# Forming the high and low parts of k at other places of an attention stage, and 25 idle products of 256 columns at its head

## The chip, the cores and the metric

The kernel runs on one core of one Trainium2 chip. The metric is the time of one execution on the device in microseconds (us), the median over repeated executions. The engines are TensorE (PE in the rows, with PEld for its weight loads), VectorE (DVE), ScalarE (ACT), GpSimd (POOL) and SyncE (SP), which here only issues transfers (DMAs).

## The reference

Three layers run one after the other in float32. The attention layer weighs with a sigmoid, not a softmax; a gated layer of eight experts and a dense layer with an exponential curve follow. This text is about the first one.

```python
# batch 4, heads 12, tokens S = 448, head size 64
scores = (q @ k.transpose) / sqrt(64) - log(S)
attn = 1 / (1 + exp(-scores))
attn_out = attn @ v
# then, on 1792 rows of 768: each row's best of 8 experts (768 -> 1024 -> 768), where x @ w_skip > 0,
# and at last (elu(x @ w_in)) @ w_out with 768 -> 2048 -> 768
```

## The kernel before, in words

**Numbers.** A float32 factor is given to TensorE as two rounded parts (type fp32r): a high part, which ScalarE casts (`split_qk`, line 239), and a low part, the rest, which VectorE subtracts (line 241). A product of two such factors takes three products of parts: high with high, high with low, low with high.

**Tiles.** Two heads lie side by side on the 128 partitions and make a pair; 4 x 6 = 24 pairs are worked through, n = 0 to 23, by the loop at line 660, with one more turn for what is left over. Two pairs make a group T: they share one load of q and of k (tiles `qr`, `kr`, `k_left`) and one set of parts: `qh`, `ql` of q and `kh`, `kl` of k, each 128 x 896 or 128 x 768, in two buffers. p = n % 2 says which pair of its group n is.

**A pair.** For each n the code runs c = 0 to 3 (line 692). At c = 0 come the scores of three blocks of 128 keys: `scores` (line 249) gives TensorE six products a block, in the order (kh, qh), (kh, ql), (kl, qh), each for two heads at once, and ScalarE the sigmoid of the block (`weigh`, line 244), which writes `at`. At c = 2 comes `mix` of the pair before (line 265): 24 or 12 float32 products into the one bank `po`; then `left_keys` (lines 281 and 291): the last 64 keys of both pairs, their sigmoid, and VectorE's copy of `po` to `xT` (line 296). At c = 3, in ten of the pairs from n = 8 on, `rows` (line 316) turns 128 finished tokens with six transposes into the tile `px`, and ScalarE copies them out (line 326). The blocks of scores, the left keys and `px` share a ring of three PSUM buffers (`pss`, line 194): what takes a buffer waits until the user three places before it was read.

**The parts of the next group** are formed in the group before it, at line 703: in the pair with p = 0 those of q, in the pair with p = 1 those of k, the high part at c = 1, the low part at c = 3. Only the first group's parts are formed ahead of the loop (lines 627 and 628).

**Beside this** VectorE rewrites 18 weight tiles of the dense layer (`narrow`, line 147: `sg`, `mg`, `mf`), six steps a tile, one, one, one and two steps at c = 0 to 3; each tile's load is issued a tile ahead (`wide_load`, line 145). From pair 19 on a generator (`sooner`, line 461) adds the small steps that choose experts; its last step is the first gather of rows by GpSimd (line 564).

**Order.** The order of TensorE, ScalarE and VectorE is the order of the code; each works through its list one by one. The transfers of SyncE and the steps of GpSimd are put in order by the planner. The loads of a group's q and k are issued one group ahead of the forming of their parts (line 680).

**The head.** `keep_warm` (line 205) gives TensorE products of zeros before any data is there: 21 of 384 columns, bfloat16.

Of the kernel before, what the change touches and what calls it, by code (L numbers as in the profile page):

```python
# [12 lines left out]
F32 = mybir.dt.float32  # L13
# [10 lines left out]
P = 128  # L24
# [67 lines left out]
def build(nc, tc, a):  # L92
# [3 lines left out]
    with ExitStack() as top:  # L96
# [80 lines left out]
        with ExitStack() as st:  # L177
# [16 lines left out]
            pss = pst.enter_context(tc.tile_pool(name="pss", bufs=3, space=PSUM))  # L194
# [7 lines left out]
            zero_b = xp.tile([P, 1, P], BF16, name="zero_b")  # L202
            nc.gpsimd.memset(zero_b, 0.0)

            def keep_warm(n):

                ps = pss.tile([P, 3, P], F32, name="idle", tag="ps")
                for _ in range(n):
                    nc.tensor.matmul(
                        ps, zero_b[:, 0], zero_b.to_broadcast([P, 3, P]), start=True, stop=True  # L210
                    )

            keep_warm(21)
            xT = xp.tile([P, NP, NT], F32, name="xT")
            lgT = xp.tile([P, RING * P], F32, name="lgT")

            def load(b, t, first=False):
                qr = qkp.tile([P, 2, S], F32, name="qr", bufs=3)
                kr = qkp.tile([P, 2, FULL * P], F32, name="kr")
                kl = qkp.tile([P, 2, LEFT], F32, name="k_left", bufs=3)  # L220
                if first:
                    for p in range(2):
                        nc.sync.dma_start(qr[:, p], q[b, t, :, p])
                        (nc.scalar, nc.sync)[p].dma_start(kr[:, p], k[b, t, :, p])
                else:
                    nc.sync.dma_start(qr, q[b, t])
                    nc.sync.dma_start(kr, k[b, t])
                nc.sync.dma_start(kl, k_left[b, t])
                return qr, kr, kl

            def split_tiles(raw):
                sizes = {"qh": S, "ql": S, "kh": FULL * P, "kl": FULL * P}
                return raw, [qkp.tile([P, 2, m], F32R, name=n) for n, m in sizes.items()]

            def split_qk(which, raw, parts, p=slice(None), hi=True, lo=True):
                r, (h, rest) = raw[which], parts[2 * which : 2 * which + 2]
                m = h.shape[2]
                if hi:
                    nc.scalar.copy(h[:, p], r[:, p, :m])
                if lo:  # L240
                    nc.vector.tensor_sub(rest[:, p], r[:, p, :m], h[:, p])

            def weigh(out, ps):
                nc.scalar.activation(out, ps, AF.Sigmoid, bias=bias, scale=QK_SCALE)  # L244
# [279 lines left out]
            def some_weights(pool, raws, splits):  # L524

                for _ in range(splits):
                    for w_t, n in ((whi_t, "whi"), (wlo_t, "wlo")):
                        w_t.append(pool.tile([P, WCH], F32R, name=f"{n}{len(w_t)}"))
                for _ in range(raws):
                    raw_t.append(pool.tile([P, WCH], F32, name=f"raw{len(raw_t)}"))  # L530
# [4 lines left out]
            def fetch(i, chunks, after=()):  # L535
                if i == NB:
                    return
                e = nc.values_load(
                    blk_e[i : i + 1, :1] if i else blk_0[:1],
                    engines=[mybir.EngineType.SP], min_val=0, max_val=E - 1,  # L540
                )
                for c in chunks:
                    src = (w1, w2)[c // 4][bass.ds(e, 1), c % 4].rearrange("o p f -> (o p) f")
                    dma = nc.sync.dma_start(raw_of(i, c), src)
                    for other in after:
                        tc.add_manual_dep(dma.ins, other.ins.name, SYNC)
# [65 lines left out]
            steps = B * NP  # L612
            raw = load(0, 0, True)
# [45 lines left out]
            nxt = None  # L659
            for n in range(steps + 1):  # L660
                b, hp = divmod(n, NP)
                T, p = divmod(n, 2)
                if n == steps - 1:
                    assert narrowed == 2 * FA
                    fetch(0, range(2))
                if n == steps:
                    qst.close()
                    wi1p = top.enter_context(tc.tile_pool(name="wi1p", reuse_waits="tile", bufs=1))
                    wi1 = wi1p.tile([P, DM], F32, name="wi1")
                    tokp = st.enter_context(tc.tile_pool(name="tokp", reuse_waits="tile", bufs=1))  # L670
                    some_weights(tokp, 2, 2)
                    fetch(0, range(2, 4), first_rows)
                    lg = logits(B - 1, None, range(KD - 2))
                if p == 0 and n < steps:
                    if n:
                        cur = nxt
                    if T + 1 < steps // 2:
                        nxt = split_tiles(nxt_raw)
                        if T + 2 < steps // 2:
                            nxt_raw = load(*divmod(T + 2, 3))  # L680
                    else:
                        nxt = None
                if p == 1 and T + 1 < steps // 2:
                    load_v(T + 1)
                at = atp.tile([P, 2 * FULL + 1, S], F32, name="at") if n < steps else None
                po = ps1.tile([P, 512], F32, name="po", tag="po") if n else None
                if m3 is not None and c0 + 1 < n:
                    nc.scalar.copy(wi0[0], m3)
                    nc.vector.tensor_sub(wi0[1], m3, wi0[0])
                    m3 = None  # L690
                turn = done_rows < LATE and hp > (b < B - 1) and (done_rows + 1) * P <= b * S
                for c in range(4):
                    now = (n, c)
                    first_splits(n, c)
                    for c2 in range(FULL):
                        if c == 0 and n < steps:
                            scores(at, c2, p, *cur[1])
                        if c == 2 and n:
                            mix(c2, n - 1, *prev, po)
                    if c == 2:  # L700
                        left_keys(n, cur, at, prev, po)
                    if nxt and n < steps and c in (1, 3):
                        split_qk(p, *nxt, hi=(c == 1), lo=(c == 3))
                    if turn and c == 3:
                        rows(done_rows)
                        done_rows += 1
                    if hp == 1 and b > 0 and c == 0:
                        logits(b - 1)
                    if hp == 1 and b > 0 and c in (2, 3):
                        m = min(4, b * S // P - done_lgt)  # L710
                        if m > 0 and b < B:
                            token_logits(done_lgt, m)
                            done_lgt += m
                    if now >= (SOON_STEP, 3):
                        for _ in range(2 + (n > SOON_STEP + 1)):
                            next(soon, None)
                    for _ in range((1, 1, 1, 2)[c] if n else 0):
                        if conv is None and narrowed < 2 * FA:
                            mf = cvp.tile([P, DM], F32, name="mf")
                            w = wides[narrowed % 2]  # L720
                            if narrowed + 1 < 2 * FA:
                                wide_load(wides[(narrowed + 1) % 2], narrowed + 1)
                            sg = cvp.tile([P, DM], I32, name="sg", bufs=1)
                            mg = cvp.tile([P, DM], I32, name="mg", bufs=1)
                            conv = narrow(mf, w, sg, mg, False)
                        if conv is not None and next(conv, 1):
                            if narrowed == 0:
                                m3, c0 = mf.rearrange("p (c f) -> p c f", c=KD), n
                            else:
                                nc.sync.dma_start((wi_d, wo_d)[narrowed % 2][narrowed // 2], mf)  # L730
                            narrowed += 1
                            conv = None
                prev = (vts.get(T), at)
# [554 lines left out]
        with ExitStack() as st:  # L1288
# [118 lines left out]
            steps = [(bi, f) for bi in range(len(blocks)) for f in range(KF2)]  # L1407
# [37 lines left out]
            for s, (bi, f) in enumerate(steps):  # L1445
# [13 lines left out]
                if bi + 1 < len(blocks):  # L1459
# [5 lines left out]
                    if f == 7:  # L1465
                        nxt = x_tiles(bi + 1)
# [55 lines left out]
```

## Time and profile before

| | us |
|---|---|
| median of three executions | 903.27 (902.49 to 905.52) |
| the profiled execution | 902.08 |
| its span, first to last instruction | 900.3 |
| PE busy in the span | 869.1 (97%) |
| DVE busy | 555.7 (62%) |
| ACT busy | 477.4 (53%) |

The attention stage fills about the first 170 us of the span; experts and dense layer fill the rest. The profile gives for every instruction its start from the beginning of the span, its duration and, where its engine sat idle before it, for how long and what ended the idle time. The mean granted TensorE clock over the span is 0.999 of full speed.

### The profile page before, as it was taken

Reading aid. Unit: us, or ns where it says so; the run is one execution under the profiler, and the core shown is the slowest. Engines: PE = TensorE matmul, PEld = TensorE weight load, DVE = VectorE, ACT = ScalarE, POOL = GpSimd, SP = SyncE. Lnnn points to the kernel's source line nnn. Section 1 sums busy time; section 2 is a strip of 40 time slices with the busy share of each in tenths; the row PEclk is TensorE's granted clock in tenths of the full one; section 3 lists DMA queues with packets and bytes.
Section 4 is the critical chain, followed back from the end, with each engine's and each line's share of the span. In section 5 each row is a group of like instructions: output and inputs, shape, how many; then the busy total and the mean of one; then the engine's idle time right before and its main releaser. Section 6 shows DMA issues by size and latency. Waiting matters only on the chain.

```text
span 900.3 us, 13676 instructions
## 1 busy us (share of the span) xinstructions
PE 869.1 (97%) x5202; PEld 703.9 (78%) x5202; DVE 555.7 (62%) x872; ACT 477.4 (53%) x680; POOL 82.1 (9%) x79
## 2 busy tenths in 40 slices
PE   8899999999999898998999999999999999999998
PEld 4444444699998787887888888888888888888997
DVE  4866767697666466885888886434344444344664
ACT  6767676555455465773545545434434434344664
POOL 1000000112110032332100000100000100000100
PEclk9999999999999999999999999999999999999999
DMA  9778785779956165955733430100000100000100
GB/s 314 260 258 298 260 308 188 258 281 410 360 187 223 55 284 216 410 203 198 245 103 96 118 106 19 71 1 18 18 18 19 71 1 1 1 1 18 54 1 36
DMA packets 37842, 134.71 MB, mean 150 GB/s; under 512 B 5082, under 2 KB 9306, under 8 KB 37746
## 3 DMA queue, kind: packets, MB, share of 16 engines
q1 hardware_dynamic: 33122, 114.26, 35.6%
q0 software_dynamic: 4480, 19.01, 5.9%
q8 instruction: 56, 0.92, 0.4%
q14 instruction: 40, 0.33, 0.1%
q10 hardware_dynamic: 144, 0.20, 0.1%
HBM read 112.47 MB, written 23.99 MB: 152 GB/s over the span
## 4 chain that ended last, share of the span: by engine, by line
PE 54%; ACT 0%; ACTq 0%; issue 0%
PE acc L1387 16%; PE pt L1387 10%; PE acc L1355 9%; PE acc L1356 9%; PE acc L1354 9%; PE acc L142 1%; PE acc L1238 0%; PE acc L588 0%; PE acc L589 0%; PE acc L590 0%; ACT raw L1398 0%; ACTq L1518 0%
## 5 line engine op out<-in xcount | busy, mean ns | idle before, releaser
L581 DVE TENSOR_TENSOR wlo<-raw,whi 128x1536 fp32r<-128x1536 f32 x64 | 111.8, 1765 | 29.6 <-ACT whi L579 24.0
L1365 DVE SCALAR_TENSOR_TENSOR m<-m,acc 128x512 f32<-128x512 f32 (+1 forms) x64 | 39.7, 620 | 139.4 <-ACT m L1364 139.4
L1363 ACT ACTIVATE m<-acc 128x512 f32<-128x512 f32 (+1 forms) x64 | 34.8, 544 | 168.6 <-PE acc L1356 158.6
L244 ACT ACTIVATE at<-ps,bias 128x896 f32<-128x896 f32 x96 | 82.4, 914 | 49.4 <-PE ps L291 30.7
L579 ACT CAST whi<-raw 128x1536 fp32r<-128x1536 f32 x64 | 94.0, 1481 | 17.0 <-PE acc L590 6.2
L1387 PE MATMUL acc<-wol,gh 128*128 128x256 f32 x320 | 100.8, 315 | 0.0
L1387 PE MATMUL acc<-woh,gl 128*128 128x256 f32 x320 | 100.4, 314 | 0.0
L1387 PE MATMUL acc<-woh,gh 128*128 128x256 f32 x320 | 100.4, 314 | 0.0
L1355 PE MATMUL acc<-x,wih 128*128 128x512 f32 (+1 forms) x270 | 96.2, 356 | 0.0
L1354 PE MATMUL acc<-x,wih 128*128 128x512 f32 (+1 forms) x270 | 96.2, 356 | 0.0
L1356 PE MATMUL acc<-x,wil 128*128 128x512 f32 (+1 forms) x270 | 96.1, 356 | 0.0
L588 PE MATMUL acc<-whi,both 128*128 128x384 f32 (+1 forms) x236 | 83.9, 355 | 2.5 <-DVE both L605 1.7
L589 PE MATMUL acc<-wlo,both 128*128 128x384 f32 (+1 forms) x236 | 82.9, 351 | 0.5 <-DVE wlo L581 0.5
L590 PE MATMUL acc<-whi,both 128*128 128x384 f32 (+1 forms) x236 | 82.5, 350 | 0.0
L1343 DVE TENSOR_TENSOR wol<-wo,woh 128x768 fp32r<-128x768 f32 x64 | 61.2, 956 | 23.4 <-ACT woh L1342 23.0
L1387 PEld LDWEIGHTS acc<-woh,gh 128*128 128x128 f32 x320 | 60.3, 188 | 10.0
L1387 PEld LDWEIGHTS acc<-wol,gh 128*128 128x128 f32 x320 | 60.3, 188 | 9.4
L1342 ACT CAST woh<-wo 128x768 fp32r<-128x768 f32 x64 | 53.3, 833 | 26.0 <-PE acc L1387 25.9
L1369 DVE TENSOR_TENSOR gl<-m,gh 128x512 fp32r<-128x512 f32 (+1 forms) x64 | 40.0, 626 | 40.5 <-ACT gh L1368 40.5
L1387 PEld LDWEIGHTS acc<-woh,gl 128*128 128x128 f32 x320 | 60.1, 188 | 4.2
L1337 DVE TENSOR_TENSOR wil<-wi,wih 128x768 fp32r<-128x768 f32 x60 | 57.4, 956 | 7.6 <-ACT wih L1336 6.9
L1368 ACT CAST gh<-m 128x512 fp32r<-128x512 f32 (+1 forms) x64 | 36.3, 567 | 45.9 <-DVE m L1365 45.9
(272 smaller groups left out, 1909.8 us busy)
## 6 DMA issues: line engine op xcount, KB each, us to landing
raw<-in_w SPq DMA_DIRECT2D x66, 768.0 KB, 12.0
raw<-in_wi SPq DMA_DIRECT2D x9, 768.0 KB, 4.2
raw<-in_wo SPq DMA_DIRECT2D x9, 768.0 KB, 6.7
raw<-in_wi SPq DMA_DIRECT2D x14, 384.0 KB
raw<-in_wo SPq DMA_DIRECT2D x14, 384.0 KB, 3.1
qr<-in_q SPq DMA_DIRECT2D x11, 448.0 KB
vt<-in_v SPq DMA_DIRECT2D x12, 384.0 KB, 5.5
x_d<-xr SPq DMA_DIRECT2D x12, 384.0 KB, 4.7
```

The lines of the kernel that those rows point to most:

```text
L244: nc.scalar.activation(out, ps, AF.Sigmoid, bias=bias, scale=QK_SCALE)
L579: nc.scalar.copy(w_hi, raw)
L581: nc.vector.tensor_sub(w_lo, raw, w_hi)
L588: nc.tensor.matmul(o, a_hi, b_hi, start=first, stop=False)
L589: nc.tensor.matmul(o, a_hi, b_lo, start=False, stop=False)
L590: nc.tensor.matmul(o, a_lo, b_hi, start=False, stop=last)
L1337: nc.vector.tensor_sub(pair[1], raw, pair[0])
L1343: nc.vector.tensor_sub(pair[1], wo_r[f], pair[0])
L1354: nc.tensor.matmul(o, a, b, start=(cc == 0), stop=False)
L1355: nc.tensor.matmul(o, a, c, start=False, stop=False)
L1356: nc.tensor.matmul(o, wil[:, cc], b, start=False, stop=(cc == KD - 1))
L1387: nc.tensor.matmul(o, a, b, start=(clears and f == 0 and k_ == 0), stop=(f == KF2 - 1 and k_ == 2), skip_group_check=True,)
```

## The change

Line 703 is replaced by a helper, `splits`. Of the next group's parts, the high part of q is cast in the first pair at c = 1 and its low part formed at c = 3, as before. The high part of k is cast in the first pair at c = 3 (it was the second pair at c = 1), and its low part is formed in the second pair at c = 1 (it was c = 3). In the first pair at c = 3 the cast of k comes ahead of the copy of turned rows in ScalarE's list. At the head 25 products of 256 columns replace the 21 of 384. Nothing else is changed.

```diff
             def keep_warm(n):
-                ps = pss.tile([P, 3, P], F32, name="idle", tag="ps")
+                ps = pss.tile([P, 2, P], F32, name="idle", tag="ps")
                 for _ in range(n):
                     nc.tensor.matmul(
-                        ps, zero_b[:, 0], zero_b.to_broadcast([P, 3, P]), start=True, stop=True
+                        ps, zero_b[:, 0], zero_b.to_broadcast([P, 2, P]), start=True, stop=True
                     )
-            keep_warm(21)
+            keep_warm(25)
...
+            def splits(now, raw, parts):
+                if now in ((0, 1), (0, 3)):
+                    split_qk(now[1] // 2, raw, parts, lo=False)
+                if now in ((0, 3), (1, 1)):
+                    split_qk(now[0], raw, parts, hi=False)
...
-                    if nxt and n < steps and c in (1, 3):
-                        split_qk(p, *nxt, hi=(c == 1), lo=(c == 3))
+                    if nxt and n < steps:
+                        splits((p, c), *nxt)
                     if turn and c == 3:
                         rows(done_rows)
```

## Rows read from the trace of the kernel before

**Rows 1.** Waits, 0 to 200 us: who waited for whom: us in total, times, longest.
```profile
DVE xT L296 <- PE ps L291: 38.0, 23, 3.2
...
PE ps L253 <- DVE kl L241: 11.8, 11, 1.5
```
**Rows 2.** Timeline from pair 3 into pair 4: start, us, engine, line, op, tiles.
```profile
27.78 0.47 PE L253 MATMUL ps<-qh,kh 64*128 64x448 f32 x2
...
27.90 0.62 DVE L296 COPY xT<-po 128x448 f32<-128x448 f32 x1 [0.46 <-PE ps L291]
...
28.09 0.37 PE L253 MATMUL ps<-ql,kh 64*128 64x448 f32 x2
...
28.91 0.95 DVE L241 TENSOR_TENSOR kl<-kr,kh 128x768 fp32r<-128x768 f32 x1
...
29.91 0.47 PE L253 MATMUL ps<-qh,kl 64*128 64x448 f32 x2 [1.46 <-DVE kl L241]
...
30.22 0.36 PE L253 MATMUL ps<-qh,kh 64*128 64x448 f32 x2
...
30.42 0.37 PE L253 MATMUL ps<-ql,kh 64*128 64x448 f32 x2
```
**Rows 3.** Timeline of pair 3, from its first scores; no rows are turned.
```profile
22.43 0.47 PE L253 MATMUL ps<-qh,kh 64*128 64x448 f32 x2
...
22.59 0.64 ACT L244 ACTIVATE at<-ps,bias 128x448 f32<-128x448 f32 x1 [0.92 <-PE ps L291]
...
23.41 2.80 ACT L244 ACTIVATE at<-ps,bias 128x896 f32<-128x896 f32 x3 [0.18 <-PE ps L253]
...
24.45 2.49 PE L265 MATMUL po<-at,vt 128*64 128x224 f32 x24
...
26.09 0.84 ACT L239 CAST kh<-kr 128x768 fp32r<-128x768 f32 x1
```
**Rows 4.** Timeline, ScalarE, where pair 8 turns rows.
```profile
61.66 0.63 ACT L244 ACTIVATE at<-ps,bias 128x448 f32<-128x448 f32 x1 [0.92 <-PE ps L291]
62.41 0.80 ACT L326 COPY xr<-px 128x768 f32<-128x768 f32 x1
```
**Rows 5.** The same stretch, TensorE: the third block of pair 9's scores.
```profile
63.62 0.36 PE L253 MATMUL ps<-qh,kh 64*128 64x448 f32 x2
```
**Rows 6.** Timeline of the head, all engines.
```profile
1.03 5.09 PE L209 MATMUL idle<-zero_b 128*128 128x384 bf16 x21 [1.03 <-POOL zero_b L203]
...
3.57 0.15 PEld L209 LDWEIGHTS <-zero_b 128*128 128x128 bf16 x1 [0.17 <-issue]
...
3.89 1.84 PEld L209 LDWEIGHTS <-zero_b 128*128 128x128 bf16 x11 [0.17 <-issue]
...
4.43 0.33 SPq L227 DMA_DIRECT2D kr<-in_k  x1
...
5.34 0.55 DVE L241 TENSOR_TENSOR kl<-kr,kh 128x384 fp32r<-128x384 f32 x1
...
6.56 0.36 PE L253 MATMUL ps<-qh,kl 64*128 64x448 f32 x2
...
10.48 3.34 ACT L244 ACTIVATE at<-ps,bias 128x448 f32<-128x448 f32 x4
...
14.08 0.56 DVE L150 TENSOR_SCALAR sg<-raw 128x768 int32<-128x768 int32 x1 [2.36 <-DMA raw<-in_wi]
...
15.63 0.36 PE L253 MATMUL ps<-ql,kh 64*128 64x448 f32 x2
```
**Rows 7.** The way out of the stage: an issue of SyncE.
```profile
159.56 0.32 SPq L730 DMA_DIRECT2D wo_d<-mf  x1
```
**Rows 8.** The same, GpSimd: the first gather of rows.
```profile
162.21 1.23 POOL L564 DMA_INDIRECT xg<-x_d,slot  x1 [8.98 <-DMA wo_d<-mf]
```
**Rows 9.** Stretch 57 to 83 us: busy PE, PEld, DVE, ACT, POOL; clock, DMA share, GB/s.
```profile
57.00:83.00 26.00, 23.89 (x170) 11.69 (x166) 18.42 (x29) 19.24 (x23) 0.00 (x0) 1.00 0.88 297
```
**Rows 10.** The tile kr: from issue to landing of its DMAs, us.
```profile
DMA to landing us min/median/max: 3.7/5.0/6.3
```

## What the change does to the time: the prediction

> **What bounds the kernel now.** Three views were read, in this order. The page's first part and the table say which engine is full: TensorE is busy 869.1 of 900.3 us, VectorE 62%, ScalarE 53%. So a microsecond of TensorE's idle time is worth about a microsecond, and the other engines count only where TensorE waits for them. The list of waits says for whom it waits in the attention stage: 11.8 us in 11 waits for VectorE's `kl`, the low part of k; VectorE in turn waits 38.0 us for TensorE, 23 times, so it has time to spare [rows 1]. Eleven is the number of changes from one group to the next (pairs 2, 4, ... 22). The timeline around one of them shows how the wait arises [rows 2]: VectorE copies `xT` at 27.90, when pair 3's left keys are done; only behind it in the list, after one more step, stands `kl` (28.91 to 29.86). TensorE has started pair 4's scores, needs `kl` for its fifth and sixth product, and stands still until 29.91.
>
> **What the wait costs.** The row gives 1.46 us of idle time. Start to start, from (kh, ql) at 28.09 to (kl, qh) at 29.91, it is 1.82 where two such steps follow each other in 0.20 (30.22 to 30.42), and the step after the restart takes 0.31 (29.91 to 30.22) where 0.20 is usual. Lost are 1.62 + 0.11 = 1.73, which is 0.27 more than the row says [rows 2]. Over eleven: 11.8 [rows 1] + 11 x 0.27 = 14.8 us.
>
> **Part 1: `kl` early in the second pair.** `kl` now stands ahead of `xT` in VectorE's list, some 4 us before TensorE wants it, and needs `kh`, which ScalarE casts at the end of the first pair. All eleven waits go: minus 14.8 us. What is late next? The step from an even pair into an odd one is the same work on TensorE without any wait for parts, and runs at 27.78 - 22.43 = 5.35 us a pair [rows 2, 3]; the other steps should now look like it. The price falls on `xT`, which now has 0.95 us more ahead of it: VectorE was idle for 0.46 us before it at 27.90, so there it comes up to 0.49 later [rows 2]. The next `mix` needs `po` free. It starts 24.45 - 22.43 = 2.02 us after a pair's first scores [rows 3], so at 27.78 + 2.02 = 29.80; `xT` would end at 27.90 + 0.62 + 0.49 = 29.01. 0.8 us of cover is left: no cost. If pairs moving up on VectorE ate that cover, each odd pair would cost what is over; the mean idle time before `xT`, 38.0 / 23 = 1.65 us, says that most pairs have more [rows 1]. The loads of k, whose buffer `kl` sets free, can only start sooner.
>
> A repeated gap can also be read otherwise. The Trainium skill (Perfetto Trace Analysis, Identifying Performance Opportunities) says that the same gap, repeating on the engine that should be full, can mean too little SBUF or PSUM for the next tile. By that the ring of three PSUM buffers would hold the scores back, the order of VectorE's list would not matter, and this part would be worth 0. The trace speaks against it here: the wait falls inside a block whose buffer is already being written, ends 0.05 us after `kl` does, and the two blocks behind it start without another one [rows 2].
>
> **Part 2: `kh` cast in the first pair.** The cast (0.84 us, [rows 3]) moves from c = 1 of the odd pair to c = 3 of the even one. Where no rows are turned, it stands between the sigmoid of the left keys (22.59) and those of the next scores (23.41 to 26.21), which end 0.7 us later; pair 3's own left keys follow at 27.9, and nobody waits for the sigmoids sooner: no cost. Where rows are turned, the copy of `px` now waits behind the cast. Ten pairs turn rows (8, 9, 10, 14 to 17, 19 to 21, by line 691's condition); five of them are even. There the sigmoid starts at 61.66 and takes 0.63, the cast 0.84, the copy 0.80 [rows 3, 4]: the end is at 63.93, or at 63.75 if each overlaps its forerunner by 0.1 as back-to-back sigmoids do (three in 2.80 us). The third block of pair 9's scores takes `px`'s place in the ring and began at 63.62 [rows 5]; it starts 0.15 to 0.35 later, and the restart costs 0.11 as above. Taken: 0.3 x 5 = plus 1.5 us. Ends: 0 (if transposes and sigmoids move apart) and 5 x 0.46 = 2.3.
>
> **Part 3: the idle products.** Spacing was 3.89 - 3.57 = 0.32 us for 384 columns, which is the 1.2 GHz level, and from 3.89 on 1.84 / 11 = 0.167, the 2.4 GHz level [rows 6]. At 256 columns that is 0.213 and 0.112. From 1.03 to 3.89 13.4 products fit; the other 11.6 take 1.3 us, to 5.2 instead of about 6.0. The first scores then meet the parts of the first half: their `kl` ends at 5.34 + 0.55 = 5.89, so the (kl, qh) products start at 5.9 instead of 6.56 [rows 6], and the sigmoids, behind which the next pair stands, move with them: 0.6 us sooner. Two thirds are given back at the first change of groups: VectorE's step at 14.08 waits for a transfer, does not move, and stands ahead of `kl`, which so runs from about 14.55 to 15.5. TensorE would want it at 15.63 + 0.20 - 0.6 = 15.2, and waits 0.3 + 0.1 [rows 6]. Taken: minus 0.2 us; ends: minus 0.6 (the transfer lands sooner) and plus 0.3 (TensorE idle between 5.2 and 5.9 makes a slow start).
>
> **The way out.** After pair 22 everything hangs on what TensorE and VectorE do, and moves with it, but for one thing: the first gather (162.21) ended its wait with the landing of a transfer issued at 159.56, 2.6 us before [rows 7, 8]. TensorE comes 1.6 us sooner at the last change of groups, VectorE's steps before `xT` of pair 22 only about 0.9 sooner (the 0.95 of `kl` less 0.1), so that the transfers ahead of it in the queue may be 0.7 late. Taken: plus 0.2; ends 0 and 0.7.
>
> **Sum.** -14.8 + 1.5 - 0.2 + 0.2 = -13.3 us, against the profiled execution's 902.08 (span 900.3 and 1.8 around it): 888.8. That execution is 1.2 us below the median of 903.27; 903.27 - 13.3 = 890.0 is the prediction. Ends of the terms: -14.8 + 0 - 0.6 + 0 = -15.4 (887.9) and -14.8 + 2.3 + 0.3 + 0.7 = -11.5 (891.8).
>
> **The rivals.**
> (a) Part of it comes back as a new wait, in the transfers or in VectorE. In 57 to 83 us the transfer engines are busy 0.88 of 26 us at 297 GB/s [rows 9]. Two waits for `kl` and two for `px` fall in it, so the same bytes get about 26 - 2.6 + 0.6 = 24.0 us: 0.95 busy. They need 0.88 x 26 = 22.9, so it fits in the mean; but a weight tile that lands late holds up VectorE, with `xT` and `kl` behind it. If that, or `xT` over its cover, takes half a microsecond in each of 11 groups, or a whole one, 5.5 to 11 us come back: 895.5 to 901. For it: the queue is near full. Against: loads are issued a tile or a group ahead. The Trainium skill (DMA: Bandwidth & Descriptors, Where 436 GB/s comes from) puts a limit of about 358 GB/s on HBM per core. By it the 7.7 MB of this stretch need 21.6 us and fit as well, so it lowers this rival's chance.
> (b) The change doesn't do what it says: the wait for `kl` only turns into one of the same length for something else that ends when `kl` did, a PSUM buffer for one. Then -0.2 to -2: 901 to 903. Only the Trainium skill's reading of the gap speaks for it; the pace of 5.35 us into odd pairs speaks against.
> (c) Slower. Asking for `kr` a pair earlier makes ScalarE stand at the cast until k lands, with the sigmoids behind it, in every group. Place: after the left keys of each even pair. The first is the nearest: `kr` issued at 4.43 lands 3.7 to 6.3 later, by 10.7; the cast comes up behind the sigmoid of 10.48, at about 11.1, or 10.5 with the head's gain [rows 6, 10]. Later groups have their load issued a group, over 10 us, ahead. It decides from 13.3 / 11 = 1.2 us of TensorE a group; at 1.7 a group the time is 903.27 + 5.5 = 908.8.
>
> **How the numbers follow.** Forecast 0.80, (a) 0.10, (b) 0.05, (c) 0.05. 0.3% is 2.7 us, about what a measurement of this kernel can tell from no change. Faster by more than that: the forecast and nearly all of (a), 0.89; within: (b) and the edge of (a), 0.06; slower: 0.05. The range goes from the low end, 887.9 less 0.9 for the scatter of the median, 887.0, up into (a) to 896.0. About 0.03 lie below it and 0.15 above.
>
> **What would show it.** Right: no wait of scores for `kl` in pairs 4 to 22; a first scores row 10.7 us after that of the same pair one group before, where no rows are turned; five waits of the third block for ScalarE's copy of `px`, 0.2 us each; the idle products ending near 5.2 and the first (kl, qh) near 5.9; from the first expert block on, every instruction about 13 us sooner with unchanged distances. Wrong: a wait of like size on another releaser at the same places, a `kh` cast ended by a transfer, `mix` waiting for `xT` in odd pairs, or the first 22 pairs shorter by 13 us and the end not.

## The result and the profile after

The changed kernel takes 889.90 us (median of four, 889.62 to 891.87), the kernel before beside it on the same chip 903.64: 13.74 us less, a ratio of 0.9851 [0.9828, 0.9873]. Predicted were 890.0. The profiled execution took 889.8 us, its span 888.0; against the profiled execution of before that is 12.3 us less. The medians differ by more because that execution of before, at 902.08, lay 1.56 below its median and this one only 0.10 below.

The first part of the page after (engine, busy us, share of the span, instructions):

```profile
PE 867.5 (98%) x5206; PEld 705.1 (79%) x5206; DVE 555.1 (63%) x872; ACT 476.3 (54%) x680; POOL 82.8 (9%) x79
```

TensorE is as busy as before to 1.6 us; what went is time in which it stood. The list of waits after, over the first 190 us, TensorE's lines and then one of VectorE's (who waits for whom: us in total, times, longest):

```profile
PE pc L142 <- DMA xg<-x_d,slot: 1.6, 1, 1.6
PE idle L209 <- POOL zero_b L203: 1.0, 1, 1.0
...
PE ps L259 <- ACT at L250: 0.5, 1, 0.5
...
DVE xT L302 <- PE ps L297: 23.3, 18, 3.2
```

The row for `kl` with its 11.8 us is gone, and no other wait of that size has come [rows 1]. VectorE's waits for TensorE fell from 38.0 us to 23.3: the work is the same, but TensorE hands it over faster. New is one wait of 1.6 us of TensorE for the first gather.

The timeline after (start, duration, engine, line, operation, out<-in, count, idle time before and what ended it): the head, pairs 3 to 4, pair 6, the turned rows between pairs 8 and 9, the gather.

```profile
1.03 4.88 PE L209 MATMUL idle<-zero_b 128*128 128x256 bf16 x25 [1.03 <-POOL zero_b L203]
...
5.84 0.47 PE L259 MATMUL ps<-qh,kh 64*128 64x448 f32 x2
...
13.15 0.56 DVE L150 TENSOR_SCALAR sg<-raw 128x768 int32<-128x768 int32 x1 [1.63 <-DMA raw<-in_wi]
...
20.59 0.62 DVE L302 COPY xT<-po 128x448 f32<-128x448 f32 x1
...
24.41 0.94 DVE L241 TENSOR_TENSOR kl<-kr,kh 128x768 fp32r<-128x768 f32 x1
...
25.85 0.47 PE L259 MATMUL ps<-qh,kh 64*128 64x448 f32 x2
26.15 0.61 DVE L302 COPY xT<-po 128x448 f32<-128x448 f32 x1
26.36 0.37 PE L259 MATMUL ps<-qh,kl 64*128 64x448 f32 x2
26.57 0.37 PE L259 MATMUL ps<-qh,kh 64*128 64x448 f32 x2
...
29.58 0.56 DVE L158 TENSOR_SCALAR mf<-mg 128x768 f32<-128x768 f32 x1 [1.88 <-DMA wo_d<-mf]
...
36.21 0.95 DVE L241 TENSOR_TENSOR kl<-kr,kh 128x768 fp32r<-128x768 f32 x1
36.84 0.36 PE L259 MATMUL ps<-ql,kh 64*128 64x448 f32 x2
37.21 0.47 PE L259 MATMUL ps<-qh,kl 64*128 64x448 f32 x2
...
55.65 0.83 ACT L239 CAST kh<-kr 128x768 fp32r<-128x768 f32 x1
56.38 0.80 ACT L332 COPY xr<-px 128x768 f32<-128x768 f32 x1
56.88 0.37 PE L259 MATMUL ps<-qh,kl 64*128 64x448 f32 x2
57.23 0.47 PE L259 MATMUL ps<-qh,kh 64*128 64x448 f32 x2
...
148.72 1.23 POOL L570 DMA_INDIRECT xg<-x_d,slot  x1 [8.34 <-DMA wo_d<-mf]
...
155.05 0.33 PE L142 MATMUL pc<-cst,xg 128*128 128x128 f32 x1
156.96 1.42 PE L142 MATMUL pc<-cst,xg 128*128 128x128 f32 x11 [1.57 <-DMA xg<-x_d,slot]
```

Pair 4: `kl` ends at 25.35 and is wanted at 26.36; TensorE runs through, where it stood for 1.46 us before [rows 2]. From here to pair 6 are 36.53 - 25.85 = 10.68 us, as forecast.

Pair 6: `kl` ends at 37.16, TensorE's product with it starts 0.37 after the one before instead of 0.20: a rest of the old wait. Its cause stands at 29.58: VectorE waited 1.88 us for the buffer of `mf`, which an earlier transfer was still reading, with everything behind it in the list.

Pairs 8 and 9: the third block of pair 9's scores starts at 57.23, 0.35 after the step before it, when the copy of `px` (56.38 to 57.18) is done. It stood behind the cast of `kh`.

The way out: the first gather is issued at 148.72, 13.49 us sooner than before [rows 8], just as far as TensorE has come. But its last rows land late, and the second product on them waits 1.57 us. Read from the same rows of both kernels, the first scores of pair 23 come 13.50 us sooner (157.25, now 143.76), the first expert block only 11.83 (171.01, now 159.18), and the end 12.3.

### The profile page after: what moved, and what is told of

Read it like the earlier page. It is cut to its first block, busy times and chain, and to the rows that moved or that the text cites. A ratio compares the mean times of both kernels' runs of the same rounds, so it can differ in the third digit from the quotient of the medians.

```text
span 888.0 us, 13671 instructions
## 1 busy us (share of the span) xinstructions
PE 867.5 (98%) x5206; PEld 705.1 (79%) x5206; DVE 555.1 (63%) x872; ACT 476.3 (54%) x680; POOL 82.8 (9%) x79
## 4 chain that ended last, share of the span: by engine, by line
PE 54%; DVE 0%; ACT 0%; issue 0%; ACTq 0%
PE acc L1393 16%; PE pt L1393 10%; PE acc L1361 9%; PE acc L1362 9%; PE acc L1360 9%; PE acc L142 1%; PE acc L1244 0%; PE acc L594 0%; PE acc L596 0%; PE acc L595 0%; DVE both L611 0%; ACT both L609 0%; ACT raw L1404 0%; ACTq L1524 0%; ACTq L609 0%
```

## The experiments

The theory: the wait came from the order of VectorE's list alone, `kl` standing behind a copy that waits for TensorE. Rivals: what counts is the cast of `kh` a pair earlier; or that k's buffer comes free sooner; or the head; or a ring of PSUM buffers. Beside the medians, the distance from the first scores of pair 0 to those of pair 23 is given as the stage: 151.20 us before, 137.92 after. It leaves out the head and the gather, whose times vary from one execution to the next. Times in us are medians, stages come from the one profiled execution of each kernel; "before" was 903.6 to 904.1 each time.

### The changed kernel again

> The changed kernel again, as the measure for the others. Theory (the order of VectorE's list: kl ahead of xT is worth all of the gain; the copy of px behind the cast costs 0.25 us in five pairs; the gather's last packets came late by chance): pair 23's first scores 13.3 to 13.7 us sooner than before, time 12.3 to 13.7 us below the kernel before; the gather from issue to its last packet takes about 6 us, as before, not the 7.7 of the first profile. Rival on the way out (the gather is late because the stage now ends sooner against the transfers): 7 to 8 us from issue to last packet again.

890.48 us, ratio 0.9861 [0.984, 0.9882]. No wait for the gather this time, and the first expert block came at 157.91, 1.27 sooner than in the first execution, yet the span (887.7) is only 0.3 shorter: that wait is not part of the change, and little of it is left at the end of these two executions. The stage is 138.78, all of the 0.86 more in pairs 0 and 1, where ScalarE waited 0.76 for a load of q (as in the head's experiment below). By that, pair 23's first scores come 12.97 us sooner than before, less than the 13.3 to 13.7 expected; the time is as expected.

### The splits alone

```diff
-                ps = pss.tile([P, 2, P], F32, name="idle", tag="ps")
+                ps = pss.tile([P, 3, P], F32, name="idle", tag="ps")
...
-            keep_warm(25)
+            keep_warm(21)
```

> The change of the parts of k alone, with the 21 idle products of 384 columns of before. Theory: eleven waits gone, five waits for px of 0.25 us, pair 23's first scores 14.6 - 1.3 = 13.3 us sooner than before, that is 0.2 us later than in the changed kernel; time 12 to 13.5 us below before. Rival (the head carries part of the gain, since all later work hangs on it): 2 us or more later than the changed kernel.

890.13 us, ratio 0.9855 [0.9835, 0.9875]; stage 137.95. The moved splits carry the whole change.

### The head alone, in the kernel before

```diff
-                ps = pss.tile([P, 3, P], F32, name="idle", tag="ps")
+                ps = pss.tile([P, 2, P], F32, name="idle", tag="ps")
...
-            keep_warm(21)
+            keep_warm(25)
```

> The 25 idle products of 256 columns alone. Theory: first scores 0.2 us sooner (0.6 if the clock rises as early as in the profile of before), all later work as before with its eleven waits; time 0 to 0.6 us below before, which can't be told from no change. Rival: 2 us or more.

904.07 us over 12 runs, ratio 1.0003 [0.9989, 1.0016]: no change that can be measured; stage 152.11. Its list of waits, and then ScalarE's timeline in pair 1:

```profile
PE ps L253 <- DVE kl L241: 11.9, 11, 1.5
```

```profile
10.47 0.94 ACT L239 CAST qh<-qr 128x896 fp32r<-128x896 f32 x1 [0.81 <-DMA qr<-in_q]
```

The waits for `kl` are those of before. ScalarE stands 0.81 us for the next q, which takes back more than the 0.12 us that the head gave (first scores at 5.93, before 6.05). It need not: in the changed kernel, and in three of its variants, ScalarE comes to this cast sooner, at 9.12 to 9.45, and q is there. What varies is when that load lands; why was not tried.

### A third buffer for k, in the kernel before

```diff
-                kr = qkp.tile([P, 2, FULL * P], F32, name="kr")
+                kr = qkp.tile([P, 2, FULL * P], F32, name="kr", bufs=3)
```

> The kernel before with three buffers for the raw k instead of two, so that no load of k waits for kl, as in the changed kernel, while kl stays where it was. Theory: nothing changes for TensorE, eleven waits for kl of the same length; time within 0.5 us of before. Rival (part of the gain came from k's loads starting sooner): 2 us or more below before.

905.10 us, ratio 1.0009 [0.9994, 1.0024]; stage 151.35; waits for `kl`: 12.1 us in 11. The 1.0 us over before can't be told from none: the interval takes in 1. That k's buffer comes free sooner is worth nothing by itself.

### The low part early, the cast kept where it was

```diff
-                        split_qk(p, *nxt, hi=(c == 1), lo=(c == 3))
+                        split_qk(p, *nxt, hi=(c == 1), lo=(c == (3 if p == 0 else 1)))
```

> The kernel before with one change: the low part of k moves from c = 3 to c = 1 of the second pair, right behind its high part, which stays there; 21 idle products as before. Theory (the place of kl ahead of xT is all that counts): the cast ends about 26.9 in pair 3, kl about 27.9, TensorE would want it at 28.3: the eleven waits go, and none for px arises, since no cast stands ahead of its copy; pair 23's first scores 14 to 14.6 us sooner than before, about 1.2 sooner than in the changed kernel; xT up to 1 us later, within its cover. Rival (the early cast is what makes it work): waits for kl of 0.5 us or more come back at most changes of groups, and the gain is 9 us or less.

890.75 us, ratio 0.9866 [0.9841, 0.989]; stage 138.17. The waits for `kl` are gone without the earlier cast, and no third block waits for `px`. Its list of waits, TensorE's and then VectorE's (from 16 to 130 us):

```profile
PE po L265 <- DVE xT L296: 1.2, 1, 1.2
...
PE ps L253 <- DVE kl L241: 0.3, 1, 0.3
...
DVE kl L241 <- ACT kh L239: 6.1, 6, 1.3
DVE mf L158 <- DMA wo_d<-mf: 2.8, 1, 2.8
```

VectorE now stands for the cast six times, 6.1 us in all, at no cost to TensorE but in pairs 5 and 6, where the wait for `mf` comes on top. What the earlier cast buys is this slack of VectorE; what it costs are the five waits for `px`. The two nearly cancel. Expected were 14 to 14.6 us off pair 23's first scores. The stage is 13.0 shorter, and what is missing are the two waits, 1.30 and 0.55 by the distances between pairs; the head took 1.26 longer here.

### The low part formed two and three times, early

```diff
-                    split_qk(now[0], raw, parts, hi=False)
+                    for _ in range(1 + 1 * now[0]):
+                        split_qk(now[0], raw, parts, hi=False)
```

For three times the line has `2 * now[0]`.

> The changed kernel with kl formed twice at its new place: 0.87 us more of VectorE in each group, ahead of xT. Theory: VectorE has 9.5 us of work in a group of 10.7, so this fills it nearly; xT comes up to 1.4 us late in odd pairs, over its cover of 0.8: waits of mix for xT of up to 0.5 us in the six groups without turned rows, 1 to 4 us in all over the changed kernel. Rival (VectorE's cover is much larger than worked out): less than 0.5 us.

> The changed kernel with kl formed three times: 1.74 us more of VectorE in each group. Theory: 11.2 us of work in a group of 10.7, VectorE becomes the bound in the groups without turned rows: 0.5 us a group at least from that, and xT over its cover by up to 1.4 us: 5 to 12 us over the changed kernel. Rival: under 3 us.

893.38 us, ratio 0.9898 [0.987, 0.9926], and 901.66, ratio 0.9968 [0.995, 0.9986]. The stages are 141.86 and 145.78: 3.94 and 7.86 more than the changed kernel's, and all of the first and 7.5 of the second have come by pair 7, not spread over the groups as expected. The waits of the kernel with three:

```profile
PE ps L260 <- DVE kl L241: 4.0, 3, 2.3
PE po L272 <- DVE xT L303: 2.9, 1, 2.9
...
DVE mf L158 <- DMA wo_d<-mf: 4.3, 1, 4.3
```

With two, VectorE has room for the step itself nearly everywhere: 3.4 of the 3.94 us come in pairs 5 and 6, behind the stand for `mf`, which grows (1.9, 3.5, 4.3 us with one, two and three; why was not followed). With three, pairs 2 and 4, ahead of that stand, cost 1.1 and 1.2 us already: there VectorE's own work is the price, and the last experiment parts the two. The median with three rose by more than the stage, by 11.8 us; in its profiled execution another 2.5 come between pair 23 and the first expert block (16.12 us against 13.63 in the changed kernel's repeat), where the granted clock was 0.50 from 156.5 to 159.8.

### The low part formed twice, at its old place

```diff
                         split_qk(p, *nxt, hi=(c == 1), lo=(c == 3))
+                        if (p, c) == (1, 3):
+                            split_qk(p, *nxt, hi=False)
```

> The kernel before with kl formed twice at its old place, behind xT. Theory (the wait is the time that VectorE's list takes from xT to the end of kl): each of the eleven waits grows by the 0.87 us of one more subtraction, pair 23's first scores come 9.6 us later than before, time 9 to 10.5 us above before. Rival (the wait is set by something that ends at about the same moment, such as a PSUM buffer): under 3 us.

921.36 us, ratio 1.0196 [1.0169, 1.0223], 17.4 more than before; in the profiled execution, with 926.24 the slowest of six, the stage is 172.79, 21.6 more. The list of waits, the timeline at pair 2, and windows (start:end, length; busy us and count of PE, PEld, DVE, ACT, POOL; granted clock; DMA share; GB/s). The third window goes from pair 8's first scores to pair 9's, the fourth from pair 10's to pair 11's:

```profile
PE ps L253 <- DVE kl L241: 22.8, 11, 2.5
```

```profile
19.65 0.47 PE L253 MATMUL ps<-qh,kl 64*128 64x448 f32 x2 [2.46 <-DVE kl L241]
...
20.85 0.58 PE L253 MATMUL ps<-qh,kh 64*128 64x448 f32 x2
21.22 0.58 PE L253 MATMUL ps<-ql,kh 64*128 64x448 f32 x2
```

```profile
17.00:20.00 3.00, 0.55 (x6) 0.34 (x6) 2.97 (x5) 0.32 (x1) 0.00 (x0) 1.00 0.93 335
20.30:23.50 3.20, 3.20 (x20) 2.13 (x18) 2.15 (x4) 3.12 (x4) 0.00 (x0) 0.50 0.88 277
64.80:74.92 10.12, 7.97 (x47) 4.00 (x46) 6.27 (x11) 4.80 (x6) 0.00 (x0) 0.83 0.66 217
81.06:89.12 8.06, 6.41 (x45) 3.15 (x44) 5.28 (x9) 5.06 (x6) 0.00 (x0) 1.00 0.91 307
8.00:180.00 172.00, 148.71 (x1009) 73.66 (x1005) 117.79 (x193) 104.72 (x124) 3.28 (x6) 0.93 0.70 236
```

The same stretch of the kernel before, up to its pair 23:

```profile
8.00:157.00 149.00, 136.67 (x997) 67.87 (x995) 107.24 (x182) 102.92 (x123) 3.37 (x6) 1.00 0.79 271
```

Eleven waits grew by 22.8 - 11.8 = 11.0 us, 1.0 each, about one step of 0.95: behind `xT` the low part's length goes to TensorE in full. That is the theory's core, and it rules out a ring of PSUM buffers, which would not know how long `kl` takes. The other 10.6 us were not expected (9 to 10.5 were, for the time). After some of the longer waits the granted clock falls to 0.50 for a time (20.3 to 23.5 us), the 1.2 GHz level; over 172 us it is 0.93, where before it was 1.00. By that some 172 x 0.07 / 0.5 = 24 us ran at half the clock, which can cost up to 12 us.

The trace parts the two prices. From pairs 10, 16, 18, 20 and 22 to the next pair the clock stays at 1.00, and these five distances grew by 0.97 to 1.02 us: the wait alone. From pairs 2, 4, 6, 8, 12 and 14 the clock falls, to a mean of 0.83 in the window of pair 8, and these six grew by 2.53 to 3.81, 16.7 in all. Of that 6 x 1.0 is the wait; the other 10.7 go with the slower clock. The times over the six executions say the same: with mean granted clocks of 0.991 to 0.993 over the span they took 919.9 to 921.4 us, with 0.985 and 0.986 they took 926.2 and 925.6.

### Turned rows ahead of the cast

```diff
-                    if nxt and n < steps:
-                        splits((p, c), *nxt)
                     if turn and c == 3:
                         rows(done_rows)
                         done_rows += 1
+                    if nxt and n < steps:
+                        splits((p, c), *nxt)
```

> The changed kernel with one exchange: at c = 3 of a pair the transposes of rows and their copy by ScalarE come ahead of the cast of k. Theory: the five steps from pairs 8, 10, 14, 16 and 20 lose their 0.25 us each, pair 23's first scores come 1.25 us sooner than in the changed kernel; no wait for kl comes back, since the cast ends only 0.8 us later and kl is not wanted for over 4 us. Time 1.2 us below the changed kernel. Rival (the 0.25 us come from something else, such as VectorE's later xT): no difference.

888.68 us, ratio 0.9843 [0.9819, 0.9866]; stage 136.74, 1.18 shorter than the changed kernel's. Timeline from pair 8 into pair 9:

```profile
55.76 0.80 ACT L332 COPY xr<-px 128x768 f32<-128x768 f32 x1
...
56.46 0.83 ACT L239 CAST kh<-kr 128x768 fp32r<-128x768 f32 x1
...
56.77 0.36 PE L259 MATMUL ps<-qh,kl 64*128 64x448 f32 x2
56.97 0.36 PE L259 MATMUL ps<-qh,kh 64*128 64x448 f32 x2
```

The third block follows after 0.20 in all five pairs: the waits for `px` came from the cast ahead of the copy, and no one misses the cast. Against the kernel before this is shown by medians; against the changed kernel the 1.2 us are seen in the stage, not resolved by the medians.

### A third buffer for `mf`, in three kernels

```diff
-                            mf = cvp.tile([P, DM], F32, name="mf")
+                            mf = cvp.tile([P, DM], F32, name="mf", bufs=3)
```

In the kernel with rows ahead of the cast, in the one with the cast kept, and in the one with three low parts:

> The changed kernel with the rows ahead of the cast of k, and with three buffers instead of two for the rewritten weight tile mf. Theory (pairs 5 and 6 are late because VectorE stands in pair 4 for 1.9 us until the first tile's transfer has landed, with xT and kl behind it): the wait for kl in pair 6 goes, the way from pair 5's to pair 7's first scores takes 10.7 us, not 11.1; pair 23 another 0.4 us sooner than with two buffers, 1.6 to 1.7 sooner than in the changed kernel; time 887 to 889. Rival: no difference, pair 6 still waits.

> The kernel before with kl moved to c = 1 behind its cast, which stays, and three buffers for mf. Theory: its wait for xT of 1.2 us in pair 5 and for kl of 0.3 in pair 6 had the same cause and go; from pair 0's to pair 23's first scores the time is that of the kernel with rows first and three buffers, within 0.3 us (136.3 us, against 151.2 before). Rival (VectorE's idle time while it waits for the late cast costs): 0.8 us or more longer.

> The changed kernel with kl formed three times, and three buffers for mf. With two buffers this cost 7.9 us over the changed kernel, all of it up to pair 8, with one wait of VectorE for a transfer of 4.3 us. Theory (the transfer's wait is most of that price; VectorE's own excess of 0.5 us a group counts in three groups only): 3 to 5 us over the changed kernel from pair 0 to pair 23. Rival (VectorE's work alone is the price): 7 us or more, as with two buffers.

889.06 us (ratio 0.9839 [0.9815, 0.9864], stage 136.58), 888.29 (0.9837 [0.9807, 0.9868], 136.32) and 896.89 (0.993 [0.9903, 0.9958], 142.24). The rest of the wait at pair 6 is gone in the first, and from pair 5 to pair 7 it takes 10.68 us, as expected; but the stage gains only 0.16 where 0.4 was expected, for in this execution a load of a weight tile came late and `kl` of pair 2 with it (0.25). The third shortens from 145.78 to 142.24: of the 7.86 us that three low parts cost, about 3.5 were the stand for `mf`, and the other 4.3 are VectorE's own work, as expected. In the second, TensorE waits for neither `kl` nor `xT` any more, with the cast still at its old place. Its timeline at pair 4:

```profile
25.76 0.96 DVE L241 TENSOR_TENSOR kl<-kr,kh 128x768 fp32r<-128x768 f32 x1 [0.52 <-ACT kh L239]
...
26.60 0.47 PE L253 MATMUL ps<-qh,kh 64*128 64x448 f32 x2
...
27.11 0.37 PE L253 MATMUL ps<-qh,kl 64*128 64x448 f32 x2
...
27.50 0.62 DVE L296 COPY xT<-po 128x448 f32<-128x448 f32 x1
```

VectorE waits 0.52 us for the cast, and `kl` is still 0.39 us ahead of TensorE (26.72 against 27.11). By the stage this is the shortest kernel of the study, 1.6 us under the changed one; by time it and the other two good ones (888.3 to 889.1) can't be told apart, nor from the changed kernel.

## Why the prediction was right, step by step

| step | predicted, us | measured, us |
|---|---|---|
| eleven group changes | -14.8 | -14.59 |
| `px` behind the cast | +1.5 | +1.27 (five of 0.25 to 0.27) |
| the head | -0.2 | -0.21 in the profiled pair; no effect by medians |
| the way out | +0.2 | +1.67 (-11.83 at the first expert block against -13.50 at pair 23) |
| the rest of the kernel | 0 | -0.45 (-12.28 in all) |
| sum, by the profiled executions | -13.3 | -12.3; by the medians -13.74 |

**Early `kl`: right.** The mechanism is shown from both sides: the length of the step is passed on in full behind `xT` (late_twice) and mostly kept from it ahead of `xT` (kl_2_times: 3.94 us for eleven steps of 0.95, 3.4 of them behind the stand for `mf`). The size was read rightly too: with the slow restart counted, 14.8 was nearer to the 14.59 measured than the 11.8 of the list of waits. The 0.27 was read from one change and taken for eleven, and it holds: in the ten without pair 6 the distance fell by 0.24 to 0.30 us more than the wait in the list. Two details failed. "All eleven waits go": pair 6 kept about 0.28 us. And `kl` is nowhere "some 4 us" ahead of TensorE: it is 1.05 and 1.0 at pairs 2 and 4, and 1.9 to 2.8 from pair 8 on. I placed VectorE's step by its place in the code. On VectorE it comes behind the `xT` of the pair before, which waits for TensorE, and the steps after it: at pair 4 `xT` starts at 20.59, and five steps follow without a pause until `kl` at 24.41. At pair 6 the stand for the buffer of `mf` comes on top. This was rival (a) in small: a late transfer with `kl` behind it, in one group instead of eleven.

**The earlier cast: right in cost, but it bought little.** The 0.25 to 0.27 us of each even turning pair lie at the low end of the 0.15 to 0.35 plus 0.11 that was given. The prediction asked what the cast would cost, and not whether it was needed; cast_kept shows that the wait goes without it.

**The head: the sum came out, its parts didn't.** The idle products ended at about 5.8 (first scores at 5.84), not near 5.2. By 0.213 and 0.112 us a product, 4.81 us make about 20 of the 25 at the slow level where 13.4 were forecast: an estimate, by which the clock rose some 1.4 us later in this execution; and nothing was given back at the first group change in the way described, for VectorE's step at 14.08 came at 13.15 with its transfer. That a transfer can take the head's gain back was right, but another one did it, q's in pair 1, and only in some executions.

**The way out: wrong step.** The prediction feared that transfers ahead of it in the queue would delay the gather's issue; 0.2 was taken, 1.67 measured up to the first expert block. The issue moved fully with TensorE (-13.49). What varied is the gather's own end: from its issue to the first expert block 8.8 us before, 10.5 after, 9.9 and 9.6 in two of the variants (waits of 1.0 and 0.7 us for `xg`), and no wait in the others, the changed kernel's repeat among them. It comes and goes with one and the same kernel; what sets it stays open. So the meeting of 890.0 and 889.90 is in part luck: the four times alone go from 889.62 to 891.87.

**The rivals.** (b), no effect, is out by the result, and its PSUM ring by late_twice. (c), k landing late, is out: in the loop no cast of `kh` waits for a transfer in the trace after (one of the first group's, ahead of it, does for 0.51 us, at 5.92). Of (a) only pair 6 is left. The bandwidth limit that the prediction set against (a) is not one here: a slice of 22.5 us of the page before moved 410 GB/s.

## What to carry to other kernels

An engine that works a list in order passes on every wait: look for a step that the full engine needs, standing behind one that waits for the full engine, and move it ahead; nothing has to become faster. Price the wait from start to start, not by the idle time in the list. Do the same reading for what the moved steps now stand ahead of (here `px`), and move only those that need it. A single early stand for a buffer can outlast the slack (1.9 us against 1.0 to 2.8 here); a third buffer there, or fewer steps behind it, shows at once whether it matters.

## What the runs showed of the hardware

- **A wait can cost twice, through the clock.** In the profiled execution of late_twice TensorE stood for `kl` eleven times. After six of the seven stands of 2.1 to 2.5 us its granted clock fell to 0.50 (the 1.2 GHz level), and the way to the next pair grew by 2.5 to 3.8 us; after the seventh (2.25 us, pair 22) and the four of 1.5 to 1.7 us it stayed at 1.00, and the way grew by 1.0. In the kernel before, with stands of 0.5 to 1.5 us, it stayed at 1.00 throughout. Waits of 11.0 us more so made the stage 21.6 us longer; by the medians (a clock of 0.991 where this execution had 0.985) the kernel is 17.4 us slower.
- **A stand costs more than its idle time.** At ten changes of groups, with 0.5 to 1.5 us in the list of waits, removing the wait gave 0.24 to 0.30 us more than the list says.
- **The clock's rise at the head is not at a fixed time.** The same 21 idle products of 384 columns took 5.09 us in the kernel before and 6.35 in cast_kept, and the first scores came at 6.05 and 7.31; the kernel's code up to there is the same.

```profile
1.03 6.35 PE L209 MATMUL idle<-zero_b 128*128 128x384 bf16 x21 [1.03 <-POOL zero_b L203]
...
7.31 0.47 PE L253 MATMUL ps<-qh,kh 64*128 64x448 f32 x2
```

  Each of the 21 that runs at the fast level saves 0.32 - 0.167 = 0.153 us [rows 6], so 1.26 us are 8 products, a rise about 2.6 us later. With fewer columns there is less to lose: the first scores came at 5.50 to 6.47 in eight profiled executions with 25 products of 256 columns, at 6.05 to 7.31 in six with 21 of 384. The Trainium skill (TensorE: Matmul & The Clock Gate, What you observe) puts the spread of that moment at 500 ns to either side; these two traces, 2.6 us apart, show more.
- **Indirect gathers end at varying times**, by up to 1.6 us of TensorE's time here, without any change of the kernel.
